# Seven half-size products for eight in the second projection of nine token pairs, with joined masks and preps

## The chip, the cores and the metric

The kernel runs on one core of a Trainium2 chip. The metric is the device time of one execution in microseconds (us); it is given as the median of several executions, beside a profile of one execution whose span is somewhat shorter than the time. A NeuronCore has four engines that compute, each with its own queue of instructions that it works off in order: TensorE (PE in the profile; its weight loads are PEld), VectorE (DVE), ScalarE (ACT) and GpSimd (POOL). A fifth, SyncE (SP), only issues transfers. Engines wait for one another by semaphores.

## The reference

A linear attention with a decaying state, for 4 batches of 8 heads of 768 tokens with 48 channels each, and behind it a two-layer perceptron with a leaky ReLU:

```python
for t in range(S):                                   # S = 768
    kt, vt, rt = k[:, :, t], v[:, :, t], r[:, :, t]
    cur = np.einsum('bhd,bhe->bhde', u[None] * kt, vt)
    y[:, :, t] = np.einsum('bhd,bhde->bhe', rt, state + cur)
    state = w[None, :, :, None] * state + np.einsum('bhd,bhe->bhde', kt, vt)
x = y.transpose(0, 2, 1, 3).reshape(B * S, H * D)    # 3072 x 384
h = x @ w_in                                         # 384 x 2048
g = np.maximum(0.01 * h, h)
out = g @ w_out                                      # 2048 x 384
```

## The kernel before

The 3072 tokens are cut into 24 tiles of 128 (`n`), six to a batch, and into twelve pairs of tiles (`m`). The attention is done tile by tile in its chunked form: products inside a tile, and a state that is carried from tile to tile.

Steps of a tile `n`, with the letters of the text `ORDER`:

- `load_one`, `load_stage` (L): k, r and v come in through GpSimd's queue, cast to bf16 (L210). Each tile has a slot of its own in `r_sb`, `k_sb`, `v_sb`.
- `prep` (P): two VectorE products, r by `qtab` (L305) and k by `ktab` (L307), that put the decay into `qk`. From tile 8 on a DMA on SP's queue turns `qk` into `tp` (L310); earlier tiles are turned on TensorE.
- `prep2` (Q): from tile 8 on three VectorE instructions, `ku` (L330), `rku` (L332) and the sum `s_tok` (L334), and then two GpSimd instructions (L342) that write the diagonal tile of the scores, `at`, from the identity and `s_tok`. Earlier tiles make `vs` (L325) instead, which `y_mm` adds through an identity matmul.
- `a_mm` (A): the scores on TensorE (L377), into two banks of PSUM. `a_mask` (M): VectorE puts them into `at` under the triangular mask, half a tile per instruction; from tile 8 on by a predicated copy over the diagonal tile (L391).
- `kv_mm` (K) on TensorE (L408) and `state` (S) on VectorE (L458, or L461 and L463) carry the state; the last tile of a batch has none.
- `y_part` (Y): y on TensorE (L493), then ScalarE copies it to `xT` (L508).

Steps of a pair `m`: `g1_pair` is the first projection of 256 tokens, in eight groups of six matmuls of 256 columns (L538), each with ScalarE's leaky ReLU into `gT` (L544). `g2` is the second projection of one tile, 16 matmuls of 384 columns that add up in one bank (L555), then a ScalarE copy to `out_sb` (L561) and a transfer out on SP's queue (L563).

The order of the instructions on every engine is the order in which the program adds them: first the text `ORDER`, then a loop over `m` from 3 to 11. One turn of it, in that order: `g1_pair(m)` eight times; `prep2` of tiles 2m+4 and 2m+5; loads of 2m+8 and 2m+9; `a_mm` and then `a_mask` of 2m+4 and 2m+5; `y_part` of 2m+2 and 2m+3; `kv_mm` and `state` of 2m+4 and 2m+5; `prep` of 2m+6 and 2m+7; `g2` of the pair before, tiles 2m-2 and 2m-1. Behind the loop stands `g2` of the last pair. Steps for tiles beyond 23 fall away, so turn 9 has no `prep`, and turns 10 and 11 have no work of VectorE at all.

`Sched.add` derives the waits from what an instruction reads (`R`) and writes (`W`). A wait for an earlier instruction of the same engine is kept only where the later one reads what the earlier one wrote, and on TensorE not at all. PSUM has eight banks; `next_bank` deals them in turn, and who writes a bank waits for the last reader of what was in it.

Of the kernel before, what the change touches and what calls it, by code (L numbers as in the profile page):

```python
# [15 lines left out]
NST = B * NC  # L16
# [104 lines left out]
def bass_rwkv5_eagle__then__act_leaky_relu_kernel(  # L121
# [20 lines left out]
    r_sb = SB("r_sb", [128, NST, HD])  # L142
    k_sb = SB("k_sb", [128, NST, HD])
    v_sb = SB("v_sb", [128, NST, H * E])
    w_row = SB("w_row", [1, HD], FP32)
    u_row = SB("u_row", [1, HD], FP32)
# [7 lines left out]
    qtab = SB("qtab", [128, HD])  # L154
    ktab = SB("ktab", [128, HD])
    tcol = SB("tcol", [128, 1], FP32)
    qexp = SB("qexp", [128, 1], FP32)
    kexp = SB("kexp", [128, 1], FP32)
# [20 lines left out]
    ps = [ctx.enter_context(nc.psum_tensor(f"ps{i}", [128, 512], FP32)) for i in range(8)]  # L179

    V, A, PE, SP, G = nc.vector, nc.scalar, nc.tensor, nc.sync, nc.gpsimd
    sch = Sched(ctx, nc)
# [3 lines left out]
    def next_bank():  # L186
        i = taken[0] % 8
        taken[0] += 1
        return ps[i], ("ps", i)
# [12 lines left out]
    def load_one(n, which, pace=()):  # L202
        b, c = divmod(n, NC)
        t0 = c * L
        src = {"k": k, "r": r, "v": v}[which][b].rearrange("h t d -> t h d")[t0:t0 + L, :, :]
        if which == "v":
            dst = v_sb[:, n, :].rearrange("p (h e) -> p h e", e=E)[:, :, 0:D]
        else:
            dst = {"k": k_sb, "r": r_sb}[which][:, n, :].rearrange("p (h d) -> p h d", d=D)
        add("pool", lambda: G.dma_start(dst, src), R=pace, W=[(which, n)], dma=f"{which}{n}")  # L210

    def load_stage(n, pace=()):
        for which in "krv":
# [80 lines left out]
    def hd(x):  # L294
        return x.rearrange("p (h d) -> p h d", d=D)

    def k_of(n):
        return k_sb[:, n, :] if n else k0_f[:, :]

    def r_of(n):  # L300
        return r_sb[:, n, :] if n else r0_f[:, :]

    def prep(n):
        iq = n % NQK
        add("dve", lambda: V.tensor_tensor(qk[iq][:, 0:H, 0:D], hd(r_of(n)), hd(qtab[:, :]), ALU.mult),  # L305
            R=[("r", n), "qtab", ("qk0", iq)], W=[("qp", iq)])
        add("dve", lambda: V.tensor_tensor(qk[iq][:, H:2 * H, 0:D], hd(k_of(n)), hd(ktab[:, :]), ALU.mult),  # L307
            R=[("k", n), "ktab", ("qk0", iq)], W=[("kp", iq)])
        if n >= TURNED:
            add("sp", lambda: SP.dma_start_transpose(tp[n % NTP][:, :, :],  # L310
                                                     qk[iq][:, :, :].rearrange("p h e -> p (h e)")),
                R=[("kp", iq), ("qp", iq), ("qk0", iq)], W=[("tp", n % NTP, 0), ("tp", n % NTP, 1)],
                dma=f"tp{n % NTP}")

    def diag(n):
        it, i2 = n % NTP, n % 4
# [3 lines left out]
    def prep2(n):  # L320
        i2, iv = n % 2, n % NVS
        if n < DIAG:
            ps_s, key = kv_bank[n]
            s_of = ps_s[:, HD:HD + H]
            add("dve", lambda: V.tensor_tensor(hd(vs[iv][:, :]),  # L325
                                               v_sb[:, n, :].rearrange("p (h e) -> p h e", e=E)[:, :, 0:D],
                                               s_of.unsqueeze(2).to_broadcast([128, H, D]), ALU.mult),
                R=[("v", n), key], W=[("vs", iv)])
        else:
            add("dve", lambda: V.tensor_tensor(ku[i2][:, :], k_of(n), u_tab[:, :], ALU.mult),  # L330
                R=[("k", n), "u_tab"], W=[("ku", i2)])
            add("dve", lambda: V.tensor_tensor(rku[i2][:, :], r_of(n), ku[i2][:, :], ALU.mult),  # L332
                R=[("r", n), ("ku", i2)], W=[("rku", i2)])
            add("dve", lambda: V.tensor_reduce(s_tok[i2][:, :], hd(rku[i2][:, :]), AX.X, ALU.add),  # L334
                R=[("rku", i2)], W=[("s", i2)])
            diag_tile(n)
# [31 lines left out]

    def a_mm(n):
        it = n % NTP  # L370
        at_bank[n] = (next_bank(), next_bank())

        def emit():
            for p in range(NP):
                for hh in range(2):
                    rows = slice(64 * hh, 64 * hh + D)
                    last = PE.matmul(at_bank[n][hh][0][:, 128 * p:128 * p + 128], tp[it][rows, NP + p, :],  # L377
                                     tp[it][rows, p, :], start=True, stop=True)
            return last

        add("pe", emit, R=[("tp", it, 0), ("tp", it, 1)], W=[key for _, key in at_bank[n]])

    def a_mask(n):
        for hh in range(2):
            part = at_bank[n][hh][0][:, :].rearrange("p (m i) -> p m i", i=128)
            if n < DIAG:
                add("dve", lambda hh=hh, part=part: V.tensor_tensor(  # L387
                    at[n % NAT][:, hh, :, :], part, mask[:, :].unsqueeze(1).to_broadcast([128, NP, 128]), ALU.mult),
                    R=[at_bank[n][hh][1], "mask"], W=[("at", n % NAT, hh)])
            else:  # L390
                add("dve", lambda hh=hh, part=part: V.copy_predicated(  # L391
                    at[n % NAT][:, hh, :, :],
                    mask[:, :].bitcast(mybir.dt.uint16).unsqueeze(1).to_broadcast([128, NP, 128]), part),
                    R=[at_bank[n][hh][1], "mask", ("at", n % NAT, hh)], W=[("at", n % NAT, hh)])

    def kv_mm(n):
        iq = n % NQK
# [68 lines left out]
    def y_mm(n, ps_y, key):  # L466
        it, ia, iv, is_ = n % NTP, n % NAT, n % NVS, n % NT

        def column(q):
            todo = []  # L470
            for s in range(NSL):
                p, kk = divmod(4 * s + q, 3)
                c0 = 128 * p
                one = []
                if kk < 2:
                    one.append((v_sb[:, n, c0 + 32 * kk:c0 + 32 * kk + 32], at[ia][:, 0, p, :]))
                if kk > 0:
# [4 lines left out]
                if n < DIAG:  # L482
                    one.append((vs[iv][:, 128 * s + 32 * q:128 * s + 32 * q + 32], ident[:, :]))
                todo += [(s, a, m, i == 0, i == len(one) - 1) for i, (a, m) in enumerate(one)]
            return todo

        def emit():
            columns = [column(q) for q in range(4)]
            for step in range(max(len(x) for x in columns)):
                for q in range(4):  # L490
                    if step < len(columns[q]):
                        s, a, m, first_mm, last_mm = columns[q][step]
                        last = PE.matmul(ps_y[32 * q:32 * q + 32, 128 * s:128 * s + 128], a, m,  # L493
                                         start=first_mm, stop=last_mm)
# [53 lines left out]
    def g2(n):  # L548
# [4 lines left out]
        def emit():  # L553
# [5 lines left out]
        add("pe", emit, R=[("gT", ig, half, j) for j in range(8)] + [("wout", i) for i in range(4)], W=[key])  # L559
        io = n % NO  # L560
        add("act", lambda: A.activation(out_sb[io][:, :], ps_o[:, 0:HD], AF.Copy),  # L561
            R=[key], W=[("o", io)])
        add("sp", lambda: SP.dma_start(out[128 * n:128 * n + 128, :], out_sb[io][:, :]),  # L563
            R=[("o", io)], W=[("out", n)], dma=f"o{io}")

    def u_table():
        ps_u, key = next_bank()
# [5 lines left out]
             "G": g1, "J": g1_pair, "H": g2, "L": lambda n: load_stage(n, pace=[("pace", (n - 4) // 2, (n - 4) % 2)])}  # L573
    for name in ORDER.split():
        steps[name[0]](*(int(x) for x in name[1:].split(".") if x))
    for m in range(FIRST // 2, NST // 2):
# [87 lines left out]
```

## Time and profile before

| | |
|---|---|
| time, median of 3 runs | 173.54 us (173.43 to 174.15) |
| span of the profiled execution | 171.8 us |
| TensorE busy | 163.4 us, 95% of the span |
| VectorE busy | 95.7 us, 56% |
| ScalarE busy | 92.5 us, 54% |
| GpSimd busy | 102.7 us, 60% |
| second projection, L555 | 384 matmuls, 64.5 us |
| masks from tile 8 on, L391 | 32 instructions, 19.8 us |
| diagonal tiles, L342 | 32 instructions, 33.8 us |

Busy time counts an instruction from its start to its end; matmuls overlap, so the distance from one start to the next is what one costs in a series. A part of the trace gives the start, the length, the engine, the line of the kernel, what is written from what, the shape, and in brackets how long the engine had been idle and who ended it. In the chain of waits the columns are start, length and what the path went through.

### The profile page before, as it was taken

The page shows a single profiled execution, that of the slowest core. Times are in us where ns is not written, and L with a number is a line of the kernel's source. Part 1 is how long each engine was busy: PE and PEld are TensorE (multiplying, and loading weights), DVE is VectorE, ACT ScalarE, POOL GpSimd, SP SyncE. Part 2 cuts the span into 40 slices and gives each one's busy share as a digit, 9 for nine tenths or more (in the row PEclk, how much of TensorE's full clock was granted, in tenths as well). Part 3 has the DMA queues.
Part 4 walks back from the last instruction along what each step waited for, and adds up shares of the span by engine and source line. Part 5 has one row for each costly group of instructions (what it writes and reads, how often), then busy time and mean ns, then how long its engine had stood idle before and what let it go on. Part 6 is the DMA issues. An engine that isn't in the chain of part 4 may idle for free.

```text
span 171.8 us, 5029 instructions
## 1 busy us (share of the span) xinstructions
PE 163.4 (95%) x2179; PEld 122.4 (71%) x2179; DVE 95.7 (56%) x209; ACT 92.5 (54%) x169; POOL 102.7 (60%) x117
## 2 busy tenths in 40 slices
PE   6799999969999989999999999999999999999993
PEld 1578799859666856876877867868868768678661
DVE  7699859550999679079189197296396520000000
ACT  4755698759123841942934934825817718539121
POOL 7999999990379998972993997957207200000000
PEclk9999999999999999999999999999999999999999
DMA  5999999999999999999499499899008011011112
GB/s 98 119 150 157 171 153 173 200 179 144 112 98 240 94 145 126 202 101 116 133 93 138 128 89 143 147 116 217 0 4 214 4 46 46 4 46 50 46 48 92
DMA packets 98970, 19.66 MB, mean 114 GB/s; under 512 B 92290, under 2 KB 98948, under 8 KB 98948
## 3 DMA queue, kind: packets, MB, share of 16 engines
q0 software_dynamic: 76512, 10.03, 89.7%
q1 hardware_dynamic: 21394, 9.11, 27.1%
q8 instruction: 17, 0.28, 0.7%
q10 hardware_dynamic: 1042, 0.20, 0.6%
q14 instruction: 5, 0.04, 0.1%
HBM read 20.45 MB, written 4.72 MB: 146 GB/s over the span
## 4 chain that ended last, share of the span: by engine, by line
PE 76%; DMA 9%; DVE 6%; POOL 6%; issue 2%; ACT 0%; POOLq 0%; ACTq 0%
PE ps L555 30%; PE ps L538 28%; PE ps L521 6%; PE ps L493 6%; DMA tp<-qk 5%; DMA w_in_sb<-in_moe_w_in_dram 4%; PE ps L377 3%; PE ps L408 2%; DVE qk L307 2%; POOL v_sb L210 2%; POOL r_sb L210 2%; POOL k_sb L210 2%; PE ps L355 1%; DVE ku L330 1%; DVE s_tok L334 1%
## 5 line engine op out<-in xcount | busy, mean ns | idle before, releaser
L555 PE MATMUL ps<-w_out_sb,gT 128*128 128x384 bf16 x384 | 64.5, 326 | 0.0
L538 PE MATMUL ps<-xT,w_in_sb 128*128 128x256 bf16 x480 | 54.5, 273 | 0.0
L555 PEld LDWEIGHTS ps<-w_out_sb,gT 128*128 128x128 bf16 x384 | 36.9, 98 | 23.4
L342 POOL TENSOR_TENSOR at<-ident,s_tok 128x512 bf16<-128x512 bf16 x32 | 33.8, 1081 | 30.3 <-DVE s_tok L334 30.3
L544 ACT ACTIVATE gT<-ps 128x512 bf16<-128x512 f32 x80 | 47.8, 597 | 7.0 <-PE ps L538 2.1
L538 PEld LDWEIGHTS ps<-xT,w_in_sb 128*128 128x128 bf16 x480 | 46.7, 98 | 6.4
L561 ACT ACTIVATE out_sb<-ps 128x384 f32<-128x384 f32 x24 | 11.8, 490 | 55.1 <-PE ps L555 55.1
L391 DVE CAST_PREDICATED at<-mask,ps 128x512 bf16<-128x512 uint16 x32 | 19.8, 684 | 27.6 <-PE ps L377 25.3
L210 POOL DMA_DIRECT2D v_sb<-in_v_dram x24 | 22.6, 948 | 0.4 <-issue 0.4
L210 POOL DMA_DIRECT2D k_sb<-in_k_dram x23 | 21.7, 945 | 0.0
L210 POOL DMA_DIRECT2D r_sb<-in_r_dram x23 | 21.4, 932 | 0.0
L508 ACT ACTIVATE xT<-ps 128x384 bf16<-128x384 f32 x24 | 11.0, 490 | 4.8 <-PE ps L493 4.3
L521 PE MATMUL ps<-xT,w_in_sb 128*128 128x128 bf16 x192 | 12.3, 219 | 0.3 <-DMA w_in_sb<-in_moe_w_in_dram 0.3
L493 PE MATMUL ps<-at,v_sb 128*32 128x128 bf16 x384 | 11.9, 224 | 0.0
L521 PEld LDWEIGHTS ps<-xT,w_in_sb 128*128 128x128 bf16 x192 | 11.1, 98 | 1.0 <-DMA w_in_sb<-in_moe_w_in_dram 0.6
L526 ACT ACTIVATE gT<-ps 128x512 bf16<-128x512 f32 x16 | 9.6, 599 | 3.6 <-PE ps L521 3.0
L332 DVE TENSOR_TENSOR rku<-r_sb,ku 128x384 bf16<-128x384 bf16 x16 | 10.8, 674 | 0.5
L387 DVE TENSOR_TENSOR at<-ps,mask 128x512 bf16<-128x512 f32 x16 | 10.3, 682 | 1.3 <-PE ps L377 1.3
L493 PEld LDWEIGHTS ps<-at,v_sb 128*32 128x32 bf16 x384 | 9.1, 98 | 2.0 <-issue 0.5
L366 ACT ACTIVATE tp<-ps 128x512 bf16<-128x512 f32 x15 | 8.2, 596 | 3.8 <-PE ps L355 3.8
L493 PE MATMUL ps<-tp,st 128*32 128x128 bf16 x240 | 10.1, 219 | 0.0
L377 PE MATMUL ps<-tp 48*128 48x128 bf16 x192 | 9.1, 228 | 0.9 <-DMA tp<-qk 0.7
(62 smaller groups left out, 134.5 us busy)
## 6 DMA issues: line engine op xcount, KB each, us to landing
out_dram<-out_sb SPq DMA_DIRECT2D x24, 192.0 KB, 2.2
v_sb<-in_v_dram POOLq DMA_DIRECT2D x24, 96.0 KB, 5.9
r_sb<-in_r_dram POOLq DMA_DIRECT2D x23, 96.0 KB, 5.1
k_sb<-in_k_dram POOLq DMA_DIRECT2D x23, 96.0 KB, 5.0
w_in_sb<-in_moe_w_in_dram POOLq DMA_DIRECT2D x4, 384.0 KB, 7.4
w_out_sb<-in_moe_w_out_dram POOLq DMA_DIRECT2D x4, 384.0 KB, 11.1
tp<-qk SPq DMA_TRANSPOSE x16, 3.4
r_f<-in_r_dram SPq DMA_DIRECT2D x1, 192.0 KB, 3.5
```

The source lines that it names most:

```text
L210: add("pool", lambda: G.dma_start(dst, src), R=pace, W=[(which, n)], dma=f"{which}{n}")
L332: add("dve", lambda: V.tensor_tensor(rku[i2][:, :], r_of(n), ku[i2][:, :], ALU.mult), R=[("r", n), ("ku", i2)], W=[("rku", i2)])
L342: add("pool", lambda hh=hh, s_of=s_of: G.tensor_tensor(at[ia][:, hh, :, :], ident[:, :].unsqueeze(1).to_broadcast([128, NP, 128]), s_of.un ...
L377: last = PE.matmul(at_bank[n][hh][0][:, 128 * p:128 * p + 128], tp[it][rows, NP + p, :], tp[it][rows, p, :], start=True, stop=True)
L391: add("dve", lambda hh=hh, part=part: V.copy_predicated(at[n % NAT][:, hh, :, :], mask[:, :].bitcast(mybir.dt.uint16).unsqueeze(1).to_broa ...
L493: last = PE.matmul(ps_y[32 * q:32 * q + 32, 128 * s:128 * s + 128], a, m, start=first_mm, stop=last_mm)
L508: add("act", lambda: A.activation(xT[m % NX][:, :, 128 * half:128 * half + 128], ps_y[:, 0:HD].rearrange("p (s t) -> p s t", t=128), AF.Copy),
L521: last = PE.matmul(ps_g[:, 128 * f:128 * f + 128], w_in_sb[:, s, 128 * fb:128 * fb + 128], xT[ix][:, s, t], start=s == 0, stop=s == NSL - 1)
L538: last = PE.matmul(ps_g[:, 256 * f:256 * f + 256], w_in_sb[:, s, 128 * fb:128 * fb + 128], xT[ix][:, s, :], start=s == 0, stop=s == NSL - 1)
L544: add("act", lambda: A.activation(gT[ig][:, 2 * j:2 * j + 2, :].rearrange("p f t -> p (f t)"), ps_g[:, :], AF.Prelu, alpha=0.01), R=[key], ...
L555: last = PE.matmul(ps_o[:, 0:HD], gT[ig][:, s, 128 * half:128 * half + 128], w_out_sb[:, s, :], start=s == 0, stop=s == NFB - 1)
L561: add("act", lambda: A.activation(out_sb[io][:, :], ps_o[:, 0:HD], AF.Copy), R=[key], W=[("o", io)])
```

## The change

Four things.

1. The second projection of pairs 3 to 11. Before, a pair is a matrix of 256 tokens by 2048, times `w_out`, 2048 by 384: with halves of tokens, of the inner dimension and of the columns that is eight block products of 128 x 1024 by 1024 x 192. `g2_seven` does it in seven, by the Strassen-Winograd scheme: `w_sum` makes four sums of blocks of `w_out` once (`tw`, in turns 3 and 4, two each), `g_sum` makes four sums of blocks of `gT` for each pair (`gs`), all on VectorE in bf16; `product` is one block product of eight matmuls of 192 columns. Several products add up in one bank, and between them ScalarE takes snapshots (`keep`) in fp32 that VectorE adds later (`plus`) to what another bank holds. Three banks are used, four in the last pair, which has an order of its own and stores half tiles.
2. From tile 8 on `prep` is one VectorE instruction over r and k, which lie beside each other now in `rk_sb`, a ring of 14 slots.
3. From tile 8 on `a_mask` is one instruction over both banks of the scores; `a_mm` skips a bank where the two would not be neighbours.
4. `y_mm` adds `vs` of tiles 0 to 7 by three matmuls of full width instead of twelve of 32 columns.

The diff, cut to its core:

```diff
-    NQK, NTP, NVS, NAT, NT, NX, NG, NO = 6, 6, 6, 6, 6, 3, 3, 4
+    NQK, NTP, NVS, NAT, NT, NX, NG, NO, NRK = 6, 6, 6, 6, 6, 3, 3, 4, 14
     TURNED, DIAG = 8, 8
+    SEVEN = (3,4,5,6,7,8,9,10,11)
+    HF, NH = NFB // 2, HD // 2
...
+    rk_sb = SB("rk_sb", [128, NRK, 2, HD])
+    r_sb, k_sb = rk_sb[:, :, 0, :], rk_sb[:, :, 1, :]
...
+    tw = [SB(f"tw{i}", [128, HF, NH]) for i in range(4)]
+    gs = [[SB(f"gs{i}_{j}", [128, HF, 128]) for j in range(4)] for i in range(2)]
+    snap = [[SB(f"snap{i}_{j}", [128, NH], FP32) for j in range(4)] for i in range(2)]
...
     def prep(n):
         iq = n % NQK
...
         if n >= TURNED:
+            both = rk_sb[:, n % NRK, :, :].rearrange("p w (h d) -> p (w h) d", d=D)
+            by = tab[:, :, :].rearrange("p w (h d) -> p (w h) d", d=D)
+            add("dve", lambda: V.tensor_tensor(qk[iq][:, :, 0:D], both, by, ALU.mult),
+                R=[("r", n % NRK), ("k", n % NRK), "qtab", "ktab", ("qk0", iq)], W=[("qp", iq), ("kp", iq)])
...
     def a_mm(n):
         it = n % NTP
+        if n >= DIAG and taken[0] % 8 == 7:
+            taken[0] += 1
         at_bank[n] = (next_bank(), next_bank())
...
     def a_mask(n):
+        if n >= DIAG:
+            i = at_bank[n][0][1][1]
+            halves = [("at", n % NAT, hh) for hh in range(2)]
+            add("dve", lambda: V.copy_predicated(
+                at[n % NAT][:, :, :, :].rearrange("p two m i -> p (two m) i"),
+                mask[:, :].bitcast(mybir.dt.uint16).unsqueeze(1).to_broadcast([128, H, 128]),
+                ps_all[:, 512 * i:512 * i + 1024].rearrange("p (m i) -> p m i", i=128)),
+                R=[key for _, key in at_bank[n]] + ["mask"] + halves, W=halves)
+            return
...
     def y_mm(n, ps_y, key):
...
-                if n < DIAG:
-                    one.append((vs[iv][:, 128 * s + 32 * q:128 * s + 32 * q + 32], ident[:, :]))
...
+            if n < DIAG:
+                for s in range(NSL):
+                    last = PE.matmul(ps_y[:, 128 * s:128 * s + 128], vs[iv][:, 128 * s:128 * s + 128], ident[:, :],
+                                     start=False, stop=s == NSL - 1)
...
+    def w_sum(i):
+        top, low = slice(0, HF), slice(HF, NFB)
+        one, two = slice(0, NH), slice(NH, HD)
+        a, b, op, keys = [
+            (w_out_sb[:, top, two], w_out_sb[:, top, one], ALU.subtract, []),
+            (w_out_sb[:, low, two], tw[0][:, :, :], ALU.subtract, [("tw", 0)]),
+            (w_out_sb[:, low, two], w_out_sb[:, top, two], ALU.subtract, []),
+            (w_out_sb[:, low, one], tw[1][:, :, :], ALU.subtract, [("tw", 1)]),
+        ][i]
+        add("dve", lambda: V.tensor_tensor(tw[i][:, :, :], a, b, op),
+            R=[("wout", j) for j in range(4)] + keys, W=[("tw", i)])
+
+    def g_sum(m, i):
+        ig, x = m % NG, gs[m % 2]
...
+        a, b, op, keys = [
+            (block(1, 0), block(1, 1), ALU.add, held(1, 0) + held(1, 1)),
+            (x[0][:, :, :], block(0, 0), ALU.subtract, [("gs", m % 2, 0)] + held(0, 0)),
+            (block(0, 0), block(1, 0), ALU.subtract, held(0, 0) + held(1, 0)),
+            (block(0, 1), x[1][:, :, :], ALU.subtract, [("gs", m % 2, 1)] + held(0, 1)),
+        ][i]
+        add("dve", lambda: V.tensor_tensor(x[i][:, :, :], a, b, op), R=keys, W=[("gs", m % 2, i)])
+
+    def g2_seven(m):
+        ig, i2 = m % NG, m % 2
+        final = m == NST // 2 - 1
+        banks = [next_bank() for _ in range(4 if final else 3)]
...
+        def product(where, left, right, first, last):
+            ps_o, key = banks[where]
...
+            def emit():
+                for s in range(HF):
+                    done = PE.matmul(ps_o[:, 0:NH], lhs[:, s, :], rhs[:, s, :], start=first and s == 0,
+                                     stop=s == HF - 1, skip_group_check=not (first and last))
+                return done
+
+            add("pe", emit, R=reads, W=[key])
+
+        def keep(where, i):
+            ps_o, key = banks[where]
+            add("act", lambda: A.activation(snap[i2][i][:, :], ps_o[:, 0:NH], AF.Copy), R=[key], W=[("snap", i2, i)])
...
+        def plain(where, r, c):
+            ps_o, key = banks[where]
+            io, cols = (2 * m + r) % NO, (one, two)[c]
+            add("act", lambda: A.activation(out_sb[io][:, cols], ps_o[:, 0:NH], AF.Copy), R=[key],
+                W=[("o", io, c)])
+            store(r, c)
+
+        def plus(where, i, r, c, after=()):
+            ps_o, key = banks[where]
+            io, cols = (2 * m + r) % NO, (one, two)[c]
+            add("dve", lambda: V.tensor_tensor(out_sb[io][:, cols], ps_o[:, 0:NH], snap[i2][i][:, :], ALU.add),
+                R=[key, ("snap", i2, i), *after], W=[("o", io, c)])
+            store(r, c)
+
+        landed = []
+        if not final:
+            product(0, (0, 0), (top, one), True, False)
+            keep(0, 0)
+            product(1, 0, 0, True, False)
+            keep(1, 1)
+            product(0, 1, 1, False, False)
+            keep(0, 2)
+            product(2, (0, 1), (low, one), True, True)
+            plus(2, 0, 0, 0)
+            product(0, 2, 2, False, False)
+            plus(0, 1, 1, 1)
+            product(1, 3, (low, two), False, True)
+            plus(1, 2, 0, 1)
+            product(0, (1, 1), 3, False, True)
+            plain(0, 1, 0)
+            return
...
     for m in range(FIRST // 2, NST // 2):
         for j in range(8):
             g1_pair(m, j)
         ahead = [n for n in (2 * m + 4, 2 * m + 5) if n < NST]
         for n in ahead:
             prep2(n)
+        if m - 1 in SEVEN:
+            for i in (0, 1, 3, 2):
+                g_sum(m - 1, i)
...
         for n in (2 * m + 6, 2 * m + 7):
             if n < NST:
                 prep(n)
-        g2(2 * m - 2)
-        g2(2 * m - 1)
-    g2(NST - 2)
-    g2(NST - 1)
+        if m < 5:
+            w_sum(2 * m - 6)
+            w_sum(2 * m - 5)
+        second(m - 1)
+    for i in (2, 0, 1, 3):
+        g_sum(NST // 2 - 1, i)
+    second(NST // 2 - 1)
```

`second(m)` calls `g2_seven(m)` for the pairs in `SEVEN` and `g2` of both tiles otherwise. In `product` a number stands for a sum (`gs` on the left, `tw` on the right), a pair for a block of `gT` or of `w_out`; its first argument is the bank.

More of the change, by code (lines that the diff above doesn't have):

```diff
@@ L208, in load_one @@
         else:
-            dst = {"k": k_sb, "r": r_sb}[which][:, n, :].rearrange("p (h d) -> p h d", d=D)
-        add("pool", lambda: G.dma_start(dst, src), R=pace, W=[(which, n)], dma=f"{which}{n}")
+            dst = {"k": k_sb, "r": r_sb}[which][:, n % NRK, :].rearrange("p (h d) -> p h d", d=D)
+        key = (which, n if which == "v" else n % NRK)
+        add("pool", lambda: G.dma_start(dst, src), R=pace, W=[key], dma=f"{which}{n}")
     def load_stage(n, pace=()):
@@ L383, in a_mask @@
     def a_mask(n):
+        if n >= DIAG:
[7 more added lines that the diff above has]
+            return
         for hh in range(2):
             part = at_bank[n][hh][0][:, :].rearrange("p (m i) -> p m i", i=128)
-            if n < DIAG:
[L387 to L394, printed above, removed]
+            add("dve", lambda hh=hh, part=part: V.tensor_tensor(
+                at[n % NAT][:, hh, :, :], part, mask[:, :].unsqueeze(1).to_broadcast([128, NP, 128]), ALU.mult),
+                R=[at_bank[n][hh][1], "mask"], W=[("at", n % NAT, hh)])
     def kv_mm(n):
@@ new lines, in g2_seven, with store @@
+    def g2_seven(m):
+        ig, i2 = m % NG, m % 2
+        final = m == NST // 2 - 1
+        banks = [next_bank() for _ in range(4 if final else 3)]
+        top, low = slice(0, HF), slice(HF, NFB)
+        one, two = slice(0, NH), slice(NH, HD)
+        def product(where, left, right, first, last):
+            ps_o, key = banks[where]
+            if isinstance(left, int):
+                lhs, reads = gs[i2][left], [("gs", i2, left)]
+            else:
+                r, c = left
+                lhs = gT[ig][:, HF * c:HF * c + HF, 128 * r:128 * r + 128]
+                reads = [("gT", ig, r, j) for j in range(4 * c, 4 * c + 4)]
+            if isinstance(right, int):
+                rhs = tw[right]
+                reads = reads + [("tw", right)]
+            else:
+                rhs = w_out_sb[:, right[0], right[1]]
+                reads = reads + [("wout", i) for i in range(4)]
+            def emit():
[7 more added lines that the diff above has]
+            add("act", lambda: A.activation(snap[i2][i][:, :], ps_o[:, 0:NH], AF.Copy), R=[key], W=[("snap", i2, i)])
+        def store(r, c):
+            n = 2 * m + r
+            io, cols = n % NO, (one, two)[c]
+            if final:
+                add("sp", lambda: SP.dma_start(out[128 * n:128 * n + 128, cols], out_sb[io][:, cols]),
+                    R=[("o", io, c)], W=[("out", n, c)], dma=f"o{io}{c}")
+            elif (n, 1 - c) in landed:
+                add("sp", lambda: SP.dma_start(out[128 * n:128 * n + 128, :], out_sb[io][:, :]),
+                    R=[("o", io, 0), ("o", io, 1)], W=[("out", n, 0)], dma=f"o{io}")
+            landed.append((n, c))
+        def plain(where, r, c):
[26 more added lines that the diff above has]
+            plain(0, 1, 0)
+            return
+        product(0, (0, 0), (top, one), True, False)
+        keep(0, 0)
+        product(3, 2, 2, True, False)
+        keep(3, 3)
+        product(2, (0, 1), (low, one), True, True)
+        plus(2, 0, 0, 0)
+        product(3, (1, 1), 3, False, True)
+        product(1, 0, 0, True, False)
+        add("dve", lambda: V.tensor_tensor(snap[i2][1][:, :], banks[1][0][:, 0:NH], snap[i2][3][:, :], ALU.add),
+            R=[banks[1][1], ("snap", i2, 3)], W=[("snap", i2, 1)])
+        product(0, 1, 1, False, True)
+        keep(0, 2)
+        plus(0, 1, 1, 1, after=[("snap", i2, 2)])
+        plus(3, 2, 1, 0)
+        product(1, 3, (low, two), False, True)
+        plus(1, 2, 0, 1)
@@ L575, in bass_rwkv5_eagle__then__act_leaky_relu_kernel, with second @@
         steps[name[0]](*(int(x) for x in name[1:].split(".") if x))
+    def second(m):
+        if m in SEVEN:
+            g2_seven(m)
+        else:
+            g2(2 * m)
+            g2(2 * m + 1)
     for m in range(FIRST // 2, NST // 2):
```

37 lines of the change are left out of this document (20 added, 17 removed).

## The prediction

> **What bounds the kernel now.** I read the chain of waits first. From 63 us on it is one engine without a gap:
>
> ```profile
> 53.12 8.41 DMA tp<-qk
> 61.53 0.14 issue
> 61.66 0.40 PE ps L377 x8
> 62.06 0.90 PE ps L493 x56
> 62.96 0.28 PE ps L408 x4
> 63.24 5.20 PE ps L555 x32
> 68.44 5.24 PE ps L538 x48
> 73.67 0.55 PE ps L377 x16
> 74.23 0.90 PE ps L493 x56
> 75.12 0.45 PE ps L408 x8
> 75.57 5.20 PE ps L555 x32
> 80.77 5.24 PE ps L538 x48
> ...
> 153.21 5.24 PE ps L538 x48
> 158.45 10.41 PE ps L555 x64
> ```
>
> A turn of the loop is L538 (5.24), the scores L377 (0.55), y L493 (0.90), KV L408 (0.45, or 0.28 where one tile has none) and the second projection L555 (5.20): 12.2 to 12.3 us. The instructions by time show VectorE and GpSimd in one turn; columns are start, length, engine and line:
>
> ```profile
> 74.12 2.48 DVE L391 CAST_PREDICATED at<-mask,ps 128x512 bf16<-128x512 uint16 x4 [5.44 <-PE ps L377]
> 79.43 0.36 DVE L332 TENSOR_TENSOR rku<-r_sb,ku 128x384 bf16<-128x384 bf16 x1
> 80.67 1.08 DVE L332 TENSOR_TENSOR rku<-r_sb,ku 128x384 bf16<-128x384 bf16 x1
> 81.79 0.55 DVE L334 TENSOR_REDUCE s_tok<-rku 128x8 f32<-128x384 bf16 x1
> 80.46 4.20 POOL L342 TENSOR_TENSOR at<-ident,s_tok 128x512 bf16<-128x512 bf16 x4 [4.20 <-DVE s_tok L334]
> ```
>
> VectorE idles 5.44 us ahead of the masks. And the same product `rku` takes 0.36 us alone, 1.08 us when one of GpSimd's diagonal tiles is running: that tile began at 80.46, the next at about 81.51 (4.20/4 each), and `rku` ended at 81.75, 0.24 behind the tile's end. Another view shows what follows when VectorE has several such products waiting:
>
> ```profile
> 45.78 1.20 DVE L307 TENSOR_TENSOR qk<-k_sb,ktab 128x384 bf16<-128x384 bf16 x1
> 46.90 1.19 DVE L330 TENSOR_TENSOR ku<-k_sb,u_tab 128x384 bf16<-128x384 bf16 x1
> 45.68 2.20 POOL L342 TENSOR_TENSOR at<-ident,s_tok 128x512 bf16<-128x512 bf16 x2 [7.33 <-DVE s_tok L334]
> ```
>
> Two tiles, two products, each held until a tile ended: they take turns.
>
> **TensorE's part.** A pair's 32 matmuls of 384 columns become 56 of 192. Per matmul the chain gives 56 ns at 128 columns (L521, 12 in 0.67), 109 at 256 (48 in 5.24), 162.5 at 384 (32 in 5.20): 0.42 ns a column plus 2.5. So 192 columns take 82.5 ns, a product of eight 0.66, seven 4.62: 0.58 less per pair, bounded by the rows at 128 and 256. The Trainium skill, "TensorE: Matmul & The Clock Gate", section "Back-to-back issue gap", speaks against it: it has pairs of weight load and matmul sustained at 81 ns for 128 columns and 131 for 512. An estimate on the line between puts 192 columns at 89 ns, a pair at 5.0 and the sum 3.3 us higher; the 56 ns above disagree, and I stay with the rows. The y steps keep their count (three wide matmuls for three rounds of four narrow ones, 0.06 each): nothing.
>
> **VectorE's part, per turn,** by spacing from one start to the next:
> - Unchanged: two prep2, 3.21 (79.05 to 82.26, the held `rku` in it); states 0.57 for a tile that starts a sequence, else 0.87, none for every sixth: 1.44, 1.74, 0.87 in turns m=4, 5, 6, then again.
> - Masks: four at 0.60 = 2.40. Joined, 1024 elements: 0.60 plus 512 at 1.04 ns = 1.13, two 2.27 (bounds 1.07 and 1.20 each).
> - Prep: 4 x 0.27 = 1.08 becomes 2 x 0.47 = 0.94 (384 more at 0.52 ns).
> - New sums `g_sum`, 1024 bf16: not in the trace. Nearest are L317 (512, 0.42) and the products of 384 (0.35), so 0.52 ns an element: 0.69. A sum that needs the one before starts after it (`ku` to `rku` 0.38 for 0.35), one that doesn't, 0.09 sooner: 0.72+0.72+0.60+0.60 = 2.64. Upper bound, the masks' rate: 4.9.
> - New `plus`, three of 192 out of PSUM: L461 takes 0.55 for 384, so 0.35, spaced 0.27: 0.81.
> - `w_sum`: 1536 elements, 0.87 each, two each in turns 3 and 4, +1.8 and +1.74.
> - ScalarE: L561 takes 0.49 for 384, so 0.33 for 192; four replace two, +0.34 of some 5 us idle. `product` 3 and 5 wait for such a copy of bank 0: 0.17 (matmul's issue to reader's start, as L377 to L391) +0.33+0.05 = 0.55 inside the 0.66 of the product between. Nothing; if the copy stayed 0.49, 0.05 twice a pair, 0.9 in all.
> - SP: transposes of the later `prep` go out about 1 us before a turn's end, land 3.4 later (the profile's table of DMA issues), and the scores ask for them 5.2 after the turn's end: hidden by some 3 us; the 8.4 of the chain above would cost 2. Loads stay two turns ahead; a ring of 14 is never waited for. Skipped banks: nothing.
>
> **Contention, c.** The sums stand right behind prep2, where GpSimd is in its second tile, and both their inputs are in SBUF like `rku`'s. No row has a sum this long beside a tile; I let them take turns, as at 45.7. The first sum waits 0.30 (82.26 to 82.56). It then holds its inputs 0.53 us, of which the tile behind it hides about 0.2 (tiles show no delay for `rku`), so that tile ends 1.38 after its predecessor, and the next sum starts 1.38 after the last instead of 0.72: +0.66 for each of tiles three and four. c = 1.62. Below, 0; if VectorE keeps all four in a row, c is 0.30 for the sums but tiles three and four end later and hold the second mask, some 0.85 on the path; above, another half tile, 2.1. The Trainium skill, "SBUF — State Buffer", section "Who interferes with whom", says the same of two SBUF inputs against a GpSimd read, as an exclusive lock for the whole instruction won by whoever starts first. The 0.36 and 1.08 agree on the wait; the tiles that `rku` left undelayed do not on the whole instruction, which would add 0.2 at each of tiles three and four.
>
> **The new wait.** Product 7 writes bank 0 after `plus` 2 has read it, and `plus` stands on VectorE's queue behind sums, masks, states and prep. All of the next turn's TensorE work is queued behind product 7. Also, by the order in which banks are dealt, products 1 or 2 and 4 reuse banks of this turn's scores and wait for the masks. So a turn lasts as long as VectorE's serial work: 3.21+2.64+1.62+2.27+0.94+0.81 = 11.49, plus states: 12.36 to 13.23, against TensorE's 11.6 to 11.76.
>
> **The sum** (end of TensorE's turn, before in brackets). Turn 3: the joined prep takes away two held instructions (L307, 1.20 each) ahead of the last transposes, so TensorE's 0.73 idle before L377 goes: 67.7 (68.44); bounds 0 and 0.73. VectorE: masks done 63.3, state, prep and two `w_sum` to 66.95. Turn 4: prep2 70.2, sums 74.4, masks 76.7, states 78.1, prep 79.1; `w_sum` 3 is done at 80.0 and product 5 waits for it; `plus` 2 at 81.4, product 7 to 82.1 (80.77). Turn 5: first mask 90.4, product 1 then, `plus` 1 at 94.2, 95.6 (92.94). Turn 6: 107.9 (105.10). 7: 120.9 (117.43). 8: 134.2 (129.60). Turn 9 has no prep, but its mask still holds product 2: 146.3 (141.77). Turn 10 is free, 5.24+0.90+4.62: 157.1 (153.21). Turn 11 and the last pair 5.24+9.24: 171.5 (168.86). The tail changes by a smaller copy and half stores, not counted. +2.7 on the profiled 171.8; the median 173.54 lies 1.74 above its span, so 176.2.
>
> **Rivals.**
> - **VectorE is not held (faster).** One mechanism: the sums pass GpSimd's tiles. At c=0, turn 4 ends 0.3 late and turns 5 to 9 run at 11.6 to 12.0: 168.2 span, 169.9. With VectorE keeping its turn (c=0.85), 172.1. It decides below c of about 1.15, as six turns each move by c. For: GpSimd's tiles do not always need the port (they hid `rku`). Against: the alternation at 45.7, and dependent sums leave gaps of 0.03 to 0.1 in which a waiting tile gets in.
> - **More contention** (c=2.1): six turns by 0.48, 179.1. For: no row shows so long a product beside a tile. Against: `rku` was released within 0.03 of its tile's end.
> - **Sums at one element a cycle:** +0.53 x4 x6 turns = 12.7, `w_sum` 4 x 0.8, about 192. Against: strided products (48 of every 64) already show 0.52 ns.
> - **Snapshots hold TensorE:** +0.9, 177.1.
> - **The products save nothing:** at 5.20/56 = 93 ns a matmul, inside the bounds 56 and 109, VectorE still sets turns 4 to 8, and turns 9 to 11 and the last pair lose 0.58 each, 178.5. The rule on the issue gap, above, points this way; its estimate of 89 ns gives 177.7. Against: three rows on one line.
>
> **Chances.** Turns taken, 0.60 (174.6 to 178); not held 0.12; VectorE keeps its turn 0.12; more contention 0.08; products or snapshots 0.05; one element a cycle 0.03. What a measurement can tell from no change is 0.5%, 172.7 to 174.4. Faster 0.22 (0.12, most of the second 0.12, a little of the first), same 0.11, slower 0.67. The range runs from the not-held case to more contention, 170.2 to 179.4, leaving one element a cycle and the tails outside; the forecast's own is 174.6 to 178.
>
> **What would show it.** The matmuls of `product` 82 ns apart; TensorE idle 0.5 to 2.7 us in each of turns 4 to 9, released by VectorE's `plus` or masks, none from turn 10; `g_sum` durations of 0.7 and above 1.2 mixed, the long ones beside L342; L342 near 1.4 where a sum precedes it; VectorE near full from 67 to 134 us. Wrong would be: all `g_sum` at 0.7 with TensorE unbroken (not held), or `g_sum` 1.2 in turns 10 and 11, where GpSimd is idle (one a cycle).

## The result, and the profile after

The changed kernel takes 178.13 us (median; 177.91 to 178.65) against 173.84 of the kernel before beside it: ratio 1.0244, interval 1.0202 to 1.0286. It is slower. Its profiled execution has a span of 176.6 us against 171.8.

The chain of waits of the changed kernel (start, length, what the path went through; its lines L558, L613, L401, L639 and L670 are first projection, `g_sum`, joined mask, `product` and `plus`):

```profile
80.17 2.20 PE ps_all L639 x24
82.37 5.24 PE ps_all L558 x48
...
88.93 0.68 DVE gs L613
89.61 2.27 DVE at L401 x2
...
94.57 0.62 DVE out_sb L670 x2
95.20 0.05 issue
95.24 0.83 PE ps_all L639 x8
96.08 5.24 PE ps_all L558 x48
...
104.22 4.29 PE ps_all L639 x48
...
116.85 4.88 PE ps_all L639 x56
...
153.90 4.79 PE ps_all L639 x56
...
163.93 8.66 PE ps_all L639 x104
```

Where one engine stood without a gap, the path now leaves TensorE in each turn with sums beside tiles. It goes through the last sum and the masks. In turn 5 (and turn 8, which looks the same) it goes on through the states and the second `plus` and comes back with product 7 alone (L639 x8 at 95.24). In the other turns it comes back earlier: in turn 4 behind a sum of the weights with the last three products (x24 at 80.17), in turns 6 and 9 behind the first mask with six (x48 at 104.22), in turn 7 behind it with all seven (x56 at 116.85). From 153.90 on no wait stands ahead of the seven products.

From the instructions by time: the start of the first matmul of the first projection in one turn to that in the next, in us; in the last column from turn 11's to the end of the span.

| turn | 3 | 4 | 5 | 6 | 7 | 8 | 9 | 10 | 11 and end |
|---|---|---|---|---|---|---|---|---|---|
| before | 13.07 | 12.34 | 12.16 | 12.17 | 12.33 | 12.17 | 12.16 | 11.44 | 18.76 |
| after | 12.33 | 14.80 | 13.71 | 12.43 | 13.23 | 13.69 | 12.34 | 10.92 | 18.08 |

Turns 4 to 9 lose 6.9 us together; turns 3, 10 and the end win 1.9. VectorE and GpSimd in turn 5 of the changed kernel (start, length, engine, line):

```profile
83.58 1.08 DVE L344 TENSOR_TENSOR rku<-rk_sb,ku 128x384 bf16<-128x384 bf16 x1
...
85.17 0.94 DVE L613 TENSOR_TENSOR gs<-gT 128x1024 bf16<-128x1024 bf16 x1
86.15 1.41 DVE L613 TENSOR_TENSOR gs<-gs,gT 128x1024 bf16<-128x1024 bf16 x1
87.59 1.42 DVE L613 TENSOR_TENSOR gs<-gT,gs 128x1024 bf16<-128x1024 bf16 x1
88.93 0.68 DVE L613 TENSOR_TENSOR gs<-gT 128x1024 bf16<-128x1024 bf16 x1
83.37 5.09 POOL L354 TENSOR_TENSOR at<-ident,s_tok 128x512 bf16<-128x512 bf16 x4 [4.75 <-DVE s_tok L346]
```

Three sums are held (0.94, 1.41 and 1.42 us) and the last, behind the fourth tile, is not (0.68): sums and tiles take turns. The four tiles last 5.09 instead of the 4.20 of the kernel before. No idle time of VectorE shows in this turn.

### The profile page after: what moved, and what is told of

Its sections match the earlier page's. It is cut to its first block, busy times and chain, and to the rows that moved or that the text cites. A ratio compares the mean times of both kernels' runs of the same rounds, so it can differ in the third digit from the quotient of the medians.

```text
span 176.6 us, 5399 instructions
## 1 busy us (share of the span) xinstructions
PE 162.1 (92%) x2323; PEld 136.4 (77%) x2323; DVE 139.3 (79%) x246; ACT 95.1 (54%) x186; POOL 108.4 (61%) x117
## 4 chain that ended last, share of the span: by engine, by line
PE 78%; DVE 12%; POOL 3%; issue 3%; ACT 1%; DVEq 0%; POOLq 0%
PE ps_all L558 30%; PE ps_all L639 17%; PE ps_all L575 9%; PE ps_all L541 7%; DVE at L401 5%; PE ps_all L508 4%; PE ps_all L391 4%; PE ps_all L367 3%; DVE gs L613 2%; POOL rk_sb L217 2%; DVE sum_t L478 2%; PE ps_all L513 1%; PE ps_all L425 1%; DVE out_sb L670 1%; DVE qk L315 1%
## 5 line engine op out<-in xcount | busy, mean ns | idle before, releaser
L558 PE MATMUL ps_all<-xT,w_in_sb 128*128 128x256 bf16 x480 | 54.5, 273 | 0.0
L564 ACT ACTIVATE gT<-ps_all 128x512 bf16<-128x512 f32 x80 | 47.8, 597 | 6.5 <-PE ps_all L558 2.5
L558 PEld LDWEIGHTS ps_all<-xT,w_in_sb 128*128 128x128 bf16 x480 | 46.7, 98 | 5.5
L639 PE MATMUL ps_all<-tw,gs 128*128 128x192 bf16 x216 | 20.8, 246 | 2.7 <-DVE tw L595 1.7
L217 POOL DMA_DIRECT2D rk_sb<-in_k_dram x23 | 21.7, 944 | 0.0
L217 POOL DMA_DIRECT2D rk_sb<-in_r_dram x23 | 21.4, 932 | 0.0
L670 DVE TENSOR_TENSOR out_sb<-ps_all,snap 128x192 f32<-128x192 f32 x28 | 9.2, 352 | 15.4 <-PE ps_all L639 14.7
L401 DVE CAST_PREDICATED at<-mask,ps_all 128x1024 bf16<-128x1024 uint16 x16 | 18.8, 1212 | 2.5 <-PE ps_all L391 2.5
L639 PEld LDWEIGHTS ps_all<-tw,gs 128*128 128x128 bf16 x216 | 17.9, 98 | 3.3 <-issue 1.9
L639 PE MATMUL ps_all<-w_out_sb,gT 128*128 128x192 bf16 x144 | 14.9, 246 | 4.6 <-DVE at L401 4.6
L575 PE MATMUL ps_all<-w_out_sb,gT 128*128 128x384 bf16 x96 | 16.4, 326 | 0.0
L639 PEld LDWEIGHTS ps_all<-w_out_sb,gT 128*128 128x128 bf16 x144 | 11.8, 98 | 5.3 <-DVE at L401 5.2
L613 DVE TENSOR_TENSOR gs<-gT 128x1024 bf16<-128x1024 bf16 x18 | 13.7, 768 | 0.0
L575 PEld LDWEIGHTS ps_all<-w_out_sb,gT 128*128 128x128 bf16 x96 | 9.1, 98 | 5.9
L541 PEld LDWEIGHTS ps_all<-xT,w_in_sb 128*128 128x128 bf16 x192 | 11.8, 101 | 0.6 <-issue 0.3
```

What stands on the lines that cost most here:

```text
L217: add("pool", lambda: G.dma_start(dst, src), R=pace, W=[key], dma=f"{which}{n}")
L401: add("dve", lambda: V.copy_predicated(at[n % NAT][:, :, :, :].rearrange("p two m i -> p (two m) i"), mask[:, :].bitcast(mybir.dt.uint16). ...
L541: last = PE.matmul(ps_g[:, 128 * f:128 * f + 128], w_in_sb[:, s, 128 * fb:128 * fb + 128], xT[ix][:, s, t], start=s == 0, stop=s == NSL - 1)
L558: last = PE.matmul(ps_g[:, 256 * f:256 * f + 256], w_in_sb[:, s, 128 * fb:128 * fb + 128], xT[ix][:, s, :], start=s == 0, stop=s == NSL - 1)
L564: add("act", lambda: A.activation(gT[ig][:, 2 * j:2 * j + 2, :].rearrange("p f t -> p (f t)"), ps_g[:, :], AF.Prelu, alpha=0.01), R=[key], ...
L575: last = PE.matmul(ps_o[:, 0:HD], gT[ig][:, s, 128 * half:128 * half + 128], w_out_sb[:, s, :], start=s == 0, stop=s == NFB - 1)
```

## The experiments

Each row names a kernel, its time beside the kernel before on the same chip, and the ratio of the two.

| kernel | us | before | ratio, interval |
|---|---|---|---|
| sums ahead of prep2 | 176.8 | 173.18 | 1.0206 (1.0171 to 1.0241) |
| short tiles | 170.94 | 173.18 | 0.9881 (0.9841 to 0.9921) |
| memset tiles | 170.59, one run | 173.18 | |
| product 7 set free | 178.12 | 173.18 | 1.0284 (1.0248 to 1.0320) |
| joined parts only | 173.0 | 173.12 | 0.9986 (0.9963 to 1.0010) |
| pairs 4, 6, 8, 9, 10 | 172.77 | 173.12 | 0.9990 (0.9953 to 1.0028) |
| last pair plain | 177.75 | 173.12 | 1.0281 (1.0233 to 1.0329) |
| pairs 8, 9, 10 | 170.9 | 173.12 | 0.9898 (0.9861 to 0.9935) |
| 4, 6, 8, 9, 10, weight sums in turn 3 | 171.4 | 173.5 | 0.9888 (0.9851 to 0.9925) |
| the same, two masks a tile | 171.73 | 173.5 | 0.9906 (0.9873 to 0.9939) |
| pairs 8, 9, 10, two masks a tile | 170.5 | 173.5 | 0.9832 (0.9802 to 0.9862) |

### Is it the tiles?

```diff
-                at[ia][:, hh, :, :], ident[:, :].unsqueeze(1).to_broadcast([128, NP, 128]),
-                s_of.unsqueeze(2).to_broadcast([128, NP, 128]), ALU.mult),
+                at[ia][:, hh, :, 0:16], ident[:, 0:16].unsqueeze(1).to_broadcast([128, NP, 16]),
+                s_of.unsqueeze(2).to_broadcast([128, NP, 16]), ALU.mult),
```

> GpSimd writes only 16 of the 128 columns of each head's diagonal tile (seven eighths of the diagonal's contribution are left out of the output); all else as in the changed kernel. Theory: without tiles of 1.05 us beside them the four sums take 2.64 instead of 4.37 and rku 0.36 instead of 1.08; VectorE's turn falls to some 9.2 us plus states, below TensorE's 11.6 to 11.8, and the loop is TensorE's again: L558 to L558 at 11.7 to 12.0 in turns 5 to 9, 171 us (170.3 to 172). Rival (VectorE's added 2.64 and 0.81 us are already too much without contention): turns 5 to 8 stay above 12.3, 175 or more.

Measured 170.94 us; turns 5 to 9 last 12.24, 11.65, 11.84, 12.24 and 11.65. All sums take 0.68 to 0.69 and every `rku` 0.36. The theory holds but for turns 5 and 8, and the rival falls. In those two turns both tiles have a state, and product 7 still starts 1.13 behind product 6 instead of 0.66: masks, states, preps and two `plus` take too long behind the scores even where nothing is held, and these turns are no shorter than before. Turn 4 still lasts 13.64, as it has the last two sums of the weights. The hold has not vanished, it has turned round; GpSimd's short tiles in one turn, the first two beside `rku`, the others beside the sums:

```profile
81.88 0.72 POOL L354 TENSOR_TENSOR at<-ident,s_tok 128x64 bf16<-128x64 bf16 x2 [6.04 <-DVE s_tok L346]
83.12 1.40 POOL L354 TENSOR_TENSOR at<-ident,s_tok 128x64 bf16<-128x64 bf16 x2 [0.51 <-DVE s_tok L346]
```

Now VectorE is the one that starts first, and the two tiles beside the sums take 0.68 longer together, 0.33 to 0.34 each.

The second form leaves the tile its size and takes its reading away:

```diff
-            add("pool", lambda hh=hh, s_of=s_of: G.tensor_tensor(
-                at[ia][:, hh, :, :], ident[:, :].unsqueeze(1).to_broadcast([128, NP, 128]),
-                s_of.unsqueeze(2).to_broadcast([128, NP, 128]), ALU.mult),
+            add("pool", lambda hh=hh, s_of=s_of: G.memset(at[ia][:, hh, :, :], 0.0),
```

> GpSimd fills the diagonal tiles with zeros (a memset that reads nothing) instead of the product of the identity and the sums (the diagonal's contribution is left out of tiles 8 to 23). If what holds VectorE is the reading of GpSimd's product, the sums and rku run at 0.7 and 0.36 us beside the memsets, and the time is that of the short tiles, some 171 us. If any GpSimd instruction over such a tile holds it, rku and the sums are still held until a memset ends.

The one execution that there is took 170.59 us. From its instructions by time:

```profile
81.31 0.36 DVE L344 TENSOR_TENSOR rku<-rk_sb,ku 128x384 bf16<-128x384 bf16 x1
82.17 0.68 DVE L611 TENSOR_TENSOR gs<-gT 128x1024 bf16<-128x1024 bf16 x1
82.89 0.69 DVE L611 TENSOR_TENSOR gs<-gs,gT 128x1024 bf16<-128x1024 bf16 x1
81.07 0.99 POOL L354 MEMSET at<- 128x512 bf16 x2 [6.62 <-DVE s_tok L346]
82.31 0.99 POOL L354 MEMSET at<- 128x512 bf16 x2 [0.26 <-DVE s_tok L346]
```

`rku` lies inside the first two memsets and is not held; the first two sums overlap the next two memsets and take 0.68 and 0.69. And the memsets beside the sums take 0.99 for two, as those before them: neither engine holds the other. The short tiles, no longer than these memsets where nothing holds them (0.33 and 0.43 against 0.53) but with inputs from SBUF, were held by the sums. So, as far as these two forms can tell, it is GpSimd's reading that makes the two take turns.

### Is it the place of the sums, or VectorE's volume?

```diff
+        if m - 1 in SEVEN:
+            for i in (0, 1, 3, 2):
+                g_sum(m - 1, i)
         for n in ahead:
             prep2(n)
-        if m - 1 in SEVEN:
-            for i in (0, 1, 3, 2):
-                g_sum(m - 1, i)
```

> The four sums of a turn stand ahead of prep2 instead of behind it, where GpSimd has no tile to write. Theory (a turn is VectorE's serial work, and 1.73 us of it is the sums taking turns with the tiles): all sums at 0.7 us, the block 4.37 becomes 2.64; but the tiles start 2.6 us later, so the second mask waits for tile four, which ends 8.25 us into VectorE's turn, and is done at 9.4 instead of 9.85. Only some 0.4 us in each of turns 4 to 9 is won: 175.6 us, 175 to 176.5. Rival (the volume of VectorE's work alone decides, contention is a detail): no change, 178.1. Second rival (contention is all of it): 1.7 in each turn, about 170.

Measured 176.8. The sums take 0.69 each, and the second mask waits for tile four, as expected; its wait in the instructions by time, and a piece of the chain a little later:

```profile
102.40 1.22 DVE L401 CAST_PREDICATED at<-mask,ps_all 128x1024 bf16<-128x1024 uint16 x1 [0.69 <-POOL at L354]
```

```profile
106.26 7.96 DMA tp<-qk
```

Turns 5, 6, 8 and 9 win 0.4 to 0.9 each on the changed kernel, 2.4 together. Two give 1.5 back. In turn 7 (13.94 for 13.23) the second scores wait 1.78 for a transpose that took 8 us to land. In turn 4 (15.61 for 14.80) TensorE waited 2.42 for the third sum of the weights, and then ran at half its clock; stretches of that turn with busy time of PE, PEld, DVE, ACT and POOL, and behind them the granted clock:

```profile
74.00:78.60 4.60, 2.18 (x28) 1.98 (x26) 4.53 (x8) 0.99 (x3) 4.60 (x6) 1.00 1.24 64
...
79.30:81.80 2.50, 2.50 (x18) 2.31 (x16) 1.61 (x6) 0.00 (x0) 0.00 (x0) 0.50 1.96 174
81.80:84.00 2.20, 2.20 (x19) 1.81 (x18) 2.17 (x4) 1.19 (x3) 0.00 (x0) 0.81 1.81 97
```

Products 6 and 7 took 1.28 instead of 0.66 each there, 1.2 us together. So the experiment bears the mechanism out and not the sum.

```diff
             product(0, 2, 2, False, False)
-            plus(0, 1, 1, 1)
+            keep(0, 3)
+            io = (2 * m + 1) % NO
+            add("dve", lambda io=io: V.tensor_tensor(out_sb[io][:, two], snap[i2][3][:, :], snap[i2][1][:, :], ALU.add),
+                R=[("snap", i2, 3), ("snap", i2, 1)], W=[("o", io, 1)])
+            store(1, 1)
```

> Product 7 no longer waits for VectorE: ScalarE snapshots bank 0 behind product 5, and VectorE adds the two snapshots later. VectorE has the same number of instructions. Theory (the volume of VectorE's serial work sets the turn): product 7 and the next first projection start up to 0.8 us earlier, and products 1 or 2 wait that much longer for the masks: 177.5 to 178.5, no change. Rival (the wait of product 7 is what costs): TensorE wins back 0.5 to 0.9 in turns 4, 5, 7 and 8, 175 to 176.

No change: 178.12. TensorE's waits, in total, times and longest (the changed kernel first, then this one):

```profile
PE ps_all L639 <- DVE at L401: 5.6, 6, 1.5
...
PE ps_all L639 <- DVE out_sb L670: 0.6, 2, 0.3
```

```profile
PE ps_all L639 <- DVE at L401: 7.2, 6, 1.6
```

Product 7 now starts 0.66 behind product 6 in every turn, where it started 1.13 behind it in turns 5 and 8. The waits for `plus` are gone and those for the masks are 1.6 us longer. A wait on a full queue that is taken away comes back at the next instruction that needs the queue; what counts is the work in it.

### The other parts

```diff
-    SEVEN = (3,4,5,6,7,8,9,10,11)
+    SEVEN = ()
...
-        if m < 5:
-            w_sum(2 * m - 6)
-            w_sum(2 * m - 5)
```

> The changed kernel with no pair in seven products and no sums of the weights; joined preps and masks, the ring and the full-width vs matmuls stay. Theory: TensorE's 0.73 us of idle ahead of the scores of tile 11 goes, and nothing else on its path: 0.7 to 0.9 less than before, 173.0. Rival (the joined parts cost by their skipped banks and later first halves): 173.8 or above.

Measured 173.0. That is the theory's number, but the kernel before took 173.12 beside it, so nothing was won: the rival. Its turn 3 is 12.34 against 13.07, the 0.73 that the theory names, but turns 5, 7 and 8 are 12.33, 12.50 and 12.33 against 12.16, 12.33 and 12.17. The distance from KV to the second projection grew by 0.16 there: the latter takes a bank that a mask reads, and the joined mask reads it to its own end. In turn 5 the mask starts at 85.50 and lasts 1.22, and the first matmul of L575 starts at 86.78.

```diff
-    SEVEN = (3,4,5,6,7,8,9,10,11)
+    SEVEN = (3,4,5,6,7,8,9,10)
```

> As the changed kernel, but the last pair goes the old way in 32 matmuls. TensorE's end moves by +0.58. In the changed kernel the last three plus stand in a row behind a snapshot and end 0.8 us behind the last product; in the old order one copy of 0.49 follows the last matmul. Theory (the last pair's gain is given back in the tail): no change, 178.0 within 0.5. Rival (the tail costs nothing): +0.6, 178.7. Other rival (half stores cost much): -0.5 or more.

Measured 177.75 (177.41 to 178.51), the same: the last pair's gain is given back behind the last product. There three `plus` stand in a row in the changed kernel:

```profile
172.61 0.33 ACT L647 ACTIVATE snap<-ps_all 128x192 f32<-128x192 f32 x1 [2.31 <-PE ps_all L639]
173.03 0.89 DVE L670 TENSOR_TENSOR out_sb<-ps_all,snap 128x192 f32<-128x192 f32 x3 [0.65 <-ACT snap L647]
```

### Where the scheme pays

`SEVEN = (8,9,10)` alone:

> Seven products in pairs 8, 9 and 10 only, in turns 9, 10 and 11, where VectorE has no prep or nothing at all. Theory: three times 0.5 to 0.58 and 0.8 of the joined parts: 171.4 (171 to 172). Rival (sums beside GpSimd's tiles cost TensorE in turn 9 whatever VectorE's slack): 172 to 172.5, with TensorE idle in turn 9.

Measured 170.9, with turn 9 at 11.65, turn 10 at 10.92 and no wait of TensorE for VectorE in the loop: the theory. The sums of turn 9 are held here too (0.94, 1.42, 1.41, then 0.68); with slack on VectorE that costs nothing. Then with every second pair as well, `SEVEN = (4,6,8,9,10)`:

> Seven products in pairs 4, 6, 8, 9 and 10 only, which fall in turns 5, 7, 9, 10 and 11; pairs 3, 5, 7 and the last go the old way. Theory (VectorE's serial work over a turn, not any one instruction, costs TensorE): in a plain turn VectorE has 8.0 to 8.5 us of work in TensorE's 12.2 and runs ahead, so that in the turn behind it prep2 and the sums are done before the scores; two turns hold 21.5 us of VectorE in 23.9 of TensorE. Each of the five pairs saves 0.5 to 0.58, the joined parts 0.8: about 170.3 (169.8 to 171). Rival (a seven turn is lost by itself, whatever stands ahead of it): turns 5 and 7 last 13.5 and the result is 173 or more.

Measured 172.77. Turn 7 lasts 11.85, as the theory has it; turn 5 lasts 13.88, as the rival. VectorE starts turn 5's prep2 at 78.97, 0.09 ahead of TensorE's turn, for behind turn 4's states stand two sums of the weights of 0.87; in turn 7 it starts 2.4 ahead. So all four weight sums went into turn 3:

```diff
-        if m < 5:
-            w_sum(2 * m - 6)
-            w_sum(2 * m - 5)
+        if m < 4:
+            for i in range(4):
+                w_sum(i)
```

> Pairs 4, 6, 8, 9 and 10 in seven products as in the alternating run, but all four sums of the weights stand in turn 3, where VectorE idles 3 us ahead of the scores, instead of two of them in turn 4. Theory (in the alternating run turn 5 was long only because the weight sums of turn 4 took the lead that VectorE needed): turn 5 falls from 13.88 to 11.7 to 12.0 as turn 7 did, some 1.1 us below the run with pairs 8 to 10 alone: 169.8 (169.2 to 170.5). Rival (turn 5 has both tiles with a state, 0.3 more than turn 7, and stays lost): 13 or more in turn 5, 171 to 172.

Measured 171.4; turn 5 falls only to 13.04. Both are the numbers of the rival, but not for its reason. VectorE has its lead (prep2 from 76.71), and TensorE waits for something else, the transposes, in its instructions by time:

```profile
85.49 0.40 PE L391 MATMUL ps_all<-tp 48*128 48x128 bf16 x8 [0.97 <-DMA tp<-qk]
```

The first scores wait 0.17 for theirs, the second 0.97. Neither account is quite right: the lead was what VectorE lacked, and then a transfer takes part of the gain. Last, two masks for each tile again, with and without pairs 4 and 6 (in `a_mask` the loop over both halves for all tiles, in `a_mm` no skip):

> As the run before, with two masks of 512 for each tile again and no skipped banks. Theory (the joined mask gives its two banks free 0.5 us later than the first half alone did, and the second projection that takes them waits 0.17 us in turns 5, 7 and 8 of the run with joined parts only): these 0.17 come back where a bank is reused, 0.2 to 0.5 in all: 169.4. Rival (VectorE's 0.13 us per turn of the joined masks are worth more): the same or up to 0.4 slower.

> Pairs 8, 9 and 10 in seven products, two masks of 512 for each tile, no skipped banks. Theory as in the run before: L558 to L558 in turns 5, 7 and 8 is 12.17, 12.33 and 12.17 again instead of 12.34, 12.50 and 12.34: 0.5 less than with joined masks, 170.4. Rival: no change, 170.9.

Measured 171.73 and 170.5. In the second, turns 5, 7 and 8 last 12.17, 12.33 and 12.17 as expected. In the first turn 5 lasts 13.43: no gain that can be told. The kernel with pairs 8, 9 and 10 and two masks has the lowest time of those that leave nothing out, 1.7% below the kernel before. Its first stage, up to turn 3, was 0.8 us shorter in the profile than in the kernel before; this stage varies from 53.8 to 55.2 us between these kernels without an edit there that explains it, so part of its lead is not accounted for. Its advantage over the joined masks is shown by the turns, not by the time: turns 3, 5, 7 and 8 are 0.7 shorter together, the first stage is 0.6 longer, and both profiles span 168.6 us.

## Why the prediction was right, and where its size was off

The direction, the place and the mechanism were as forecast: turns 4 to 9 become VectorE's, the sums and GpSimd's tiles take turns, and product 7 and the masks' banks pass the delay on to TensorE. The time came out 4.3 us above the kernel before instead of 2.7. At 178.13 it lies just above the 174.6 to 178 that the forecast gave to turns taken, and nearer to the 179.1 of "more contention" than to its own 176.2. It is not that rival, for c came out near the forecast (1.73, not 2.1); by an estimate, 0.11 in each of six turns, c is some 0.7 us of the miss. By steps:

- **Seven products:** 4.62 was forecast for a pair. In turn 10 the products start 0.66 apart as forecast, only product 7 starts 0.71 behind product 6: it waits for `plus` 2, which the sum left out there. Undisturbed pairs took 4.68 to 4.79 in the chains. So a matmul of 192 columns takes the 82.5 ns of the rows, not 89 or 93. For 89 the prediction has two prices, 3.3 us more and, among the rivals, 177.7, which is 1.5 more; only the second fits a sum in which VectorE sets turns 4 to 8.
- **VectorE's terms:** in turn 5 prep2 took 3.21 (forecast 3.21), the sums 4.37 (4.26), masks 2.26 (2.27), states 1.83 (1.74), prep 0.94 (0.94), `plus` 0.80 (0.81). c was 1.73 instead of 1.62.
- **The rule of the Trainium skill**, "SBUF — State Buffer", section "Who interferes with whom": that two SBUF inputs contend with GpSimd's reads and not with its mere writes is what the memsets show (0.36 and 0.68 beside them). Who starts first holds the other, in both directions: VectorE's sums by up to 0.72 us, the short tiles by 0.33 to 0.34 each. The forecast's 0.2 of hiding was too much: tiles three and four of a turn last 1.49 instead of 1.04, 0.45 more behind a sum instead of 0.33. Its ground, that the tiles show no delay for `rku`, came from a mean (4.20/4). Singly, in the kernel before, the tile behind `rku` lasts 1.15 and the two after it 1.04, so `rku` delays it by 0.1, and the prediction's objection to the whole instruction is weaker than it was put.
- **The turns:** by the sum, turns 4 to 9 last 14.4, 13.5, 12.3, 13.0, 13.3 and 12.1; measured 14.80, 13.71, 12.43, 13.23, 13.69 and 12.34. These 1.6 us are the larger part of the miss. VectorE's own turns 5 to 8, from the first `ku` of one to that of the next, took 13.41, 12.64, 13.29 and 13.42 for the forecast 13.23, 12.36, 12.93 and 13.23. That is 1.0 together, as much as TensorE's turns 5 to 8 are longer. In turn 5 it is c and the states; in turns 6 and 7 the third `plus` also waited some 0.2 for product 6. In turn 4 the sum of the weights that product 5 needs ended at 80.03, as forecast (80.0), but product 5 started 0.14 behind it, and the turn had begun 0.1 sooner. The 0.2 of turn 9 was not taken apart.
- **The tail**, "not counted" in the forecast, is the other term that was mis-sized: from the end of turn 10 on 17.4 us were forecast (157.1 to 174.5) and 17.9 measured (158.69 to 176.6). `plus` and the snapshot behind the last products are on the path, and the run with a plain last pair shows that they cost what the seven products save.
- **Turn 3** gained 0.74 for the forecast 0.73. That the joined mask would hold a bank longer, at 0.17 in three turns of the run with joined parts only, was not in the forecast ("Skipped banks: nothing" looked at the skip only). In the changed kernel this hides in VectorE's wait.
- **The rivals:** "not held" is what the short and the memset tiles make of the kernel, 170.9 and 170.6 for the forecast 169.9; so its price was sound and its condition was absent. Snapshots did not hold TensorE: products 3 and 5 of turn 10 start 0.66 behind the ones ahead of them.

## What to carry to other kernels

Work saved on the bounding engine is worth only the slack of the engine that pays for it, turn by turn: the same trade won 0.5 us a pair where VectorE idled and lost up to 1.5 a turn where its queue was full (2.5 in turn 4, with sums of the weights). Look where the paying engine's new instructions stand in time beside those of the engine with which it takes turns; and when a wait on a full queue is removed, expect it at the next consumer of that queue. A joined instruction frees its inputs only at its end: whoever reuses the first half's buffer waits for the second.

## What the runs showed of the hardware

A VectorE product of two SBUF inputs is held by a GpSimd product over SBUF tiles (0.36 to 1.08, 0.69 to 1.42), holds one itself if it comes first, and is not held by a GpSimd memset over the same tile. A pause of 2.42 us, in a stretch where TensorE was busy 2.18 us of 4.60, was followed by 3.4 us at a granted clock of 0.50 (from 79.2 to 82.6), which is 1.7 us of clock lost. The longest pause of the changed kernel behind its start, 1.66 us, had no such sequel (1.00 throughout), nor had one of 1.78 us in the same run as the 2.42. The Trainium skill, "TensorE: Matmul & The Clock Gate", section "Part 1: The HAM clock gate (the "warmup" mystery)", has the clock halve after an idle window of about 3.4 us that runs free of the kernel; this pause was shorter, but the window's own place is not in the trace. The transposes on SP's queue took 3.4 us (median; 3.1 to 8.4) from issue to landing in the kernel before and 5.4 (3.2 to 7.0) in the changed one; why most of them became slower was not tried, and in two experiments they took the place of the wait that had been removed.
